# A reordered opening, tiled key transposes for the first unit, and counted filler products in a three-stage attention and MoE kernel

## The chip, the cores and the metric

The kernel runs on one core of one Trainium2 chip. The metric is the device time of one launch in microseconds (us); the time before is 801.66 us, the median of three runs (801.65 to 803.63). TensorE is called PE in the profile, VectorE DVE, ScalarE ACT, GpSimd POOL, and SP is the engine that issues nearly all DMAs.

## The reference

Three stages follow each other: a gated linear attention over 4 batches, 8 heads, 768 steps and head size 48; a feed-forward stage with `h*cos(h)` of width 2048; and a second one with a maximum over three products of width 768.

```python
# stage 1, per batch and head, step t (state is 48x48)
state = alpha[t][:, None] * state + outer(k[t], v[t])
y[t]  = q[t] @ state
# x = y of all heads side by side: 3072 tokens x 384
h = x @ w_in                      # 384 -> 2048
x = (h * cos(h)) @ w_out          # 2048 -> 384
h = maximum(maximum(x @ w1, x @ w2), x @ w3)   # 384 -> 768
out = h @ w_out2                  # 768 -> 384
```

## The kernel before

The 3072 tokens are worked in six units of 512 (`NU = 6`, `HB = 512`; eight chunks of 64 steps, two per batch). A unit has four pairs of heads; what the text calls a head below is one such pair, and unit 0 takes the last pair first.

`att(u, k, p, t0)` does one head of a unit in chunked form. Two scans on DVE make products of alpha: `g` backwards (L382 for unit 0, in two halves; L393 for the others) and its counterpart forwards (L388, L398), with a reciprocal between. POOL multiplies keys (L384, L397) and queries (L400) by them. PE transposes the keys (L405), ACT copies the transpose out (L408), PE makes the chunk scores (L417) and the key-value sums (L422), the scores are masked with the triangle `tri` (unit 0: ACT L429 and POOL L430; others: DVE L433), DVE updates the state (L443, L454; L440, L441), and `values` multiplies masked scores by values (L462) and queries by states (L469). A fp32 number is fed to the later stages as a high part and a low part (`fp32r`): ACT writes the high part (L498), and the low part is the remainder, made in unit 0 by a product with minus identity that adds to the PSUM bank (L501, then ACT L503), elsewhere by a DVE subtraction (L505). `pick` (L477) puts rows of the first head into the free rows 48 to 63 of the other three heads of unit 0.

`moe1(i)` is one of 96 tiles of the first feed-forward stage (16 per unit). Nine products in three groups of three, high by high, high by low, low by high (L525, L526, L527), make a 128x512 tile of `h`; ACT and DVE form `h*cos(h)` (L533, L534, L535, then L537 or L541), its high part (L538, L542) and low part (POOL L539 for tiles 0 to 19, DVE L547 from tile 20); and nine products in three groups (L552, L553, L554) add it to three PSUM accumulators `acc`. At the end of a unit each accumulator goes out through one buffer `yy`: ACT L561, DVE L562, a DMA, and only then the next. The accumulator can be used by the next unit once L562 has read it.

`weight(...)` brings a block of weights: a DMA of 384 KB of float64, ACT L322, DVE L323, the high part on ACT L327, and the low part on POOL (L331) or, for the blocks named in `LOD`, on DVE out of PSUM (L329). There are 32 blocks for the first feed-forward stage, alternating `w_in` and `w_out`.

The order of the instructions is not written by hand. Every operation is entered with an engine, a duration, what it reads and writes, and a due time. `Program.order` replays this list as a schedule, taking at each step the engine that is free first and its ready operation with the smallest due time, and the kernel is issued in that order; each engine then works its own queue in order and waits on semaphores. The table of constants at the head (`LIMIT`, `GLP1`, `LOD`, `W1E`, `ATT0`, `ATTS` and so on) and the duration formulas set due times, bank limits and engines.

Of the kernel before, what the change touches and what calls it, by code (L numbers as in the profile page):

```python
# [9 lines left out]
F32 = mybir.dt.float32  # L10
# [16 lines left out]
P = 128  # L27
C = 64
# [26 lines left out]
LIMIT = {"h": 3, "a": 3, "t": 1, "w": 1, "r": 2, "y": 2, "r0": 4}  # L55


RYS = 9
# [3 lines left out]
GLP1 = 20  # L62
# [15 lines left out]
WARM, COLD, IDLE = 16, 7.0, 2.5  # L78


class Program:
# [15 lines left out]
    def op(self, eng, dur, fn, reads=(), writes=(), due=0.0, nbytes=None, port=False):  # L97
# [19 lines left out]
        self.ops.append((eng, dur, nbytes, fn, sorted(deps), due, port))  # L117
        return n

    def order(self, banks, limit):  # L120
# [19 lines left out]
        free = dict.fromkeys(engines, 0.0)  # L140
# [8 lines left out]
        cold = COLD  # L149
        never = float("inf")  # L150
# [14 lines left out]
        for _ in range(n):  # L165
            t, e = min((max(free[e], min(map(ready, w))), e) for e, w in waiting.items() if w)
# [3 lines left out]
            _, dur, nbytes, _, _, _, port = self.ops[i]  # L170
            start[i] = t
            if e == "PE":
                if t - free[e] > IDLE:
                    cold = t + COLD
                dur += min(dur, max(0.0, cold - t) / 2)
            free[e] = t + dur
            end = t + dur
            if port:
                port_free = end
            if nbytes is not None:  # L180
                dma_free = max(dma_free, end + (0.65 if e == "SP" else 1.05)) + nbytes / 260e3
# [61 lines left out]
def tile_kernel(ctx, tc, aa, qk, vv, wt, outT):  # L243
# [29 lines left out]
    half_pi = mp.tile([P, 104], F32, name="pad1")[:, 0:1]  # L273
# [4 lines left out]
    v_b = [ap.tile([P, N2, 2, UP], F32, name=f"v{i}") for i in range(NV)]  # L278
# [30 lines left out]
    def weight(block, hi, lo, whi, wlo, due, extra=(), early=2.0):  # L309
# [4 lines left out]
        if wide:  # L314
# [6 lines left out]
            op("SP", HW, lambda: nc.sync.dma_start(raw[:, 1:1 + 4 * WB], wt[block].bitcast(U16)), (), [rk], due - early, dma(P * WB * 8))  # L321
# [30 lines left out]
    def att(u, k, p, t0):  # L352
# [6 lines left out]
        if u == 0 and k == 2:  # L359
            v, vk = q_b[2].rearrange("p (i j e) -> p i j e", i=N2, j=2), ("q", 2)  # L360
            kq_, kk_ = q_3.rearrange("p a b -> p (a b)")[0:PR, 0:2 * HB], "q01"
# [11 lines left out]
        op("SP", HW, lambda: nc.sync.dma_start(t, aa[u, p, :, 0:KO]), (), [kf], t0 - 4, dma(PR * KO * 4))  # L373
        op("SP", HW, lambda: nc.sync.dma_start(kq_, qk[u, p]), (), [kk, kq], t0 - 3.9, dma(PR * 2 * HB * 4))
        op("SP", HW, lambda: nc.sync.dma_start(v, vv[u, p]), (), [vk], t0 - 3, dma(P * HB * 4))
# [36 lines left out]
        def akmm():  # L412
            for i in range(N2):
                for h in range(2):
                    for j in range(2):
                        c, w = 2 * i + h, slice(UP * j, UP * j + D)
                        pe.matmul(r[j][C * h:C * (h + 1), AO + i * C:AO + (i + 1) * C], kv3[w, c], qv3[w, c], start=True, stop=True)  # L417
            for i in range(N2):
                for h in range(2):
                    for j in range(2):  # L420
                        w = UP if j == 0 else D
                        pe.matmul(r[h][UP * j:UP * j + w, i * D:(i + 1) * D], kt[C * h:C * (h + 1), i, UP * j:UP * j + w],  # L422
                                  v[C * h:C * (h + 1), i, j, 0:D], start=True, stop=True)

        op("PE", 2 * SWITCH + N2 * mm4(C) + N2 * mm4(D), akmm, [kk, kq, tk, vk, ("done", n2)], rk, t0 + 0.2)
# [18 lines left out]
        half = [slice(UP * h, UP * h + D) for h in range(2)]  # L444
# [11 lines left out]
        yks, y = ([("acc", 0), ("acc", 1)], acc[:2]) if u == 0 else psum2("r" if u <= RYS else "y")  # L456

        def values():
            for i in range(N2):
                for h in range(2):  # L460
                    for j in range(2):
                        pe.matmul(y[h][UP * j:UP * (j + 1), i * C:(i + 1) * C], v[C * h:C * (h + 1), i, j], a[C * h:C * (h + 1), j, i],  # L462
                                  start=(i == 0), stop=False, skip_group_check=True)
# [7 lines left out]
        picks = u == 0 and p < NP - 1  # L471

        def pick():
            for x in range(2):
                for h in range(2):
                    cs = slice(HB // 2 * h, HB // 2 * (h + 1))
                    pe.matmul(y[h][:, 0:HB // 2], sel[:, p], yy_b[0][:, x, cs], start=False, stop=False, skip_group_check=True)  # L477

        if picks:
            values_, values = values, lambda: (values_(), pick())  # L480
        op("PE", 2 * SWITCH + N2 * mm4(C) + N2 * mm4(C) + (0.7 if picks else 0.0), values,
           [*([("sel",), *[("yy0", x, h) for x in "hl" for h in range(2)]] if picks else []), vk, ("a", n2, 0), ("a", n2, 1), *[(dk, h) for h in range(0 if u else 1, 2)], *[("z", n2, h) for h in range(0 if u else 1, 2)], kq, kk], [*yks, ("done", n2)], t0 + 0.3)
# [12 lines left out]
        for h in range(2):  # L495
# [4 lines left out]
            if u < XLE:  # L500
                op("PE", 0.2, lambda h=h, cs=cs: pe.matmul(y[h][:, 0:HB // 2], minus, o()[:, 0, cs], start=False, stop=True, skip_group_check=True),  # L501
# [15 lines left out]
    def moe1(i):  # L517
# [17 lines left out]
        op("Act", act(HB), lambda: se.activation(q, q, AF.Sin, bias=half_pi), ["half pi"], [qk], m)  # L535
# [99 lines left out]
    def build():  # L635
# [17 lines left out]
        op("Pool", 1.0, lambda: make_identity(nc, ident), (), ["ident"], due=-99)  # L653
        def sine():
            ve.memset(half_pi, 0.5 * math.pi)
            se.activation(tri[:, 0, 0:1], half_pi, AF.Sin)

        op("Act", 1.4, sine, (), ["half pi", "tri"], due=-100)
# [19 lines left out]
        def warm():  # L678
            for _ in range(WARM):
                pe.matmul(acc[0][:, 0:P], ident, ident, start=True, stop=True)  # L680

        op("PE", 0.213 * WARM, warm, ["ident"], [("acc", 0)], due=-99)
# [120 lines left out]
```

## Time and profile before

| | before |
|---|---|
| median of three runs | 801.66 us |
| profiled execution, device time | 799.91 us |
| its span, first to last instruction | 798.2 us |
| PE busy | 778.7 us (98%) |
| DVE, ACT, POOL busy | 424.3, 359.6, 159.2 us |
| mean granted PE clock | 0.994 |
| moved by DMA | 71.44 MB, 90 GB/s |

A row of the timeline gives start, duration, engine, line, output and inputs, shapes, count, and in brackets the idle time before it with what ended it. Durations of matmuls overlap: the price of one in a dense stretch is the distance between two starts. Busy time counts work and not waits, and PE counts as busy while a matmul is in flight.

### The profile page before, as it was taken

The numbers are of one execution on the slowest core, as the hardware profiler recorded it, in microseconds if no ns is written. First come the engines' busy times: TensorE is split into PE (matmuls) and PEld (weight loads), VectorE is DVE, ScalarE is ACT, GpSimd is POOL, SyncE is SP. The second block draws the span as 40 slices with busy tenths as digits, with TensorE's granted clock in tenths as the row PEclk, the third lists the DMA queues.
The fourth block names the chain that finished last, engine by engine and source line by source line (L and its number), as shares of the span: only waits on it lengthen the run. The fifth ranks groups of instructions, "written<-read, shape, count | busy, mean of one in ns | idle before, by whom it ended". The sixth has DMA issues, their size and how long they took to land. (4 is left out here: it accounts for less than half of the span.)

```text
span 798.2 us, 14884 instructions
## 1 busy us (share of the span) xinstructions
PE 778.7 (98%) x6180; PEld 632.7 (79%) x6180; DVE 424.3 (53%) x701; ACT 359.6 (45%) x688; POOL 159.2 (20%) x155
## 2 busy tenths in 40 slices
PE   7899999999999999999999899999999999999998
PEld 7676777888788878878877688888888888888886
DVE  7689879756874686566567444532132222223221
ACT  5777757545654565455677344521111211112111
POOL 6667775301220122011233000200000000000000
PEclk9989999999999999999999999999999999999999
DMA  9668644501340143013256200502020110200001
GB/s 290 197 200 238 197 115 142 152 12 39 120 135 3 49 134 101 1 38 117 74 152 210 88 1 0 191 31 88 27 80 27 54 53 28 79 27 14 13 27 39
DMA packets 26466, 71.44 MB, mean 90 GB/s; under 512 B 3392, under 2 KB 3392, under 8 KB 26400
## 3 DMA queue, kind: packets, MB, share of 16 engines
q1 hardware_dynamic: 26400, 70.51, 27.9%
q8 instruction: 48, 0.79, 0.4%
q14 instruction: 18, 0.15, 0.1%
HBM read 54.37 MB, written 14.16 MB: 86 GB/s over the span
## 5 line engine op out<-in xcount | busy, mean ns | idle before, releaser
L552 PE MATMUL acc<-gh,woh 128*128 128x512 f32 x288 | 116.3, 404 | 2.6 <-DVE yy L562 2.2
L525 PE MATMUL ps<-xt,wih 128*128 128x512 f32 x288 | 116.0, 403 | 0.3 <-ACT wih L327 0.3
L554 PE MATMUL acc<-gl,woh 128*128 128x512 f32 x288 | 114.3, 397 | 0.5 <-POOL gl L539 0.5
L527 PE MATMUL ps<-xt,wil 128*128 128x512 f32 x288 | 113.3, 393 | 1.1 <-POOL wil L331 1.1
L553 PE MATMUL acc<-gh,wol 128*128 128x512 f32 x288 | 112.9, 392 | 0.0
L526 PE MATMUL ps<-xt,wih 128*128 128x512 f32 x288 | 112.8, 392 | 0.0
L535 ACT ACTIVATE q<-q,pad 128x512 f32<-128x512 f32 x96 | 69.3, 722 | 47.0 <-DVE q L534 46.8
L534 DVE SCALAR_TENSOR_TENSOR q<-q,ps 128x512 f32<-128x512 int32 x96 | 65.5, 683 | 37.3 <-ACT q L533 36.9
L613 DVE TENSOR_TENSOR ps<-t,ps 128x512 f32<-128x512 f32 x36 | 25.1, 696 | 104.4 <-PE ps L605 104.2
L533 ACT ACTIVATE q<-ps 128x512 int32<-128x512 f32 x96 | 57.0, 594 | 45.6 <-PE ps L527 44.9
L541 DVE TENSOR_TENSOR ps<-q,ps 128x512 f32<-128x512 f32 x76 | 52.8, 694 | 42.6 <-ACT q L535 42.1
L547 DVE TENSOR_TENSOR gl<-ps,gh 128x512 fp32r<-128x512 f32 x76 | 52.3, 689 | 42.9 <-ACT gh L542 42.5
L614 ACT ACTIVATE h<-ps 128x512 fp32r<-128x512 f32 x36 | 21.5, 598 | 109.7 <-DVE ps L613 109.7
L552 PEld LDWEIGHTS acc<-gh,woh 128*128 128x128 f32 x288 | 54.4, 189 | 16.2 <-DVE yy L562 4.2
L554 PEld LDWEIGHTS acc<-gl,woh 128*128 128x128 f32 x288 | 54.4, 189 | 15.7 <-DVE gl L547 2.5
L527 PEld LDWEIGHTS ps<-xt,wil 128*128 128x128 f32 x288 | 54.3, 189 | 14.2 <-POOL wil L331 2.6
L542 ACT ACTIVATE gh<-ps 128x512 fp32r<-128x512 f32 x76 | 45.1, 593 | 43.3 <-DVE ps L541 38.4
L525 PEld LDWEIGHTS ps<-xt,wih 128*128 128x128 f32 x288 | 54.5, 189 | 12.3 <-ACT wih L327 0.8
L611 DVE TENSOR_TENSOR t<-t,ps 128x512 f32<-128x512 f32 x36 | 24.7, 687 | 71.5 <-PE ps L605 70.8
L526 PEld LDWEIGHTS ps<-xt,wih 128*128 128x128 f32 x288 | 54.5, 189 | 10.3
L553 PEld LDWEIGHTS acc<-gh,wol 128*128 128x128 f32 x288 | 54.4, 189 | 10.3
L631 ACT ACTIVATE y<-ps 128x512 f32<-128x512 f32 x18 | 10.8, 597 | 93.2 <-PE ps L628 93.2
(151 smaller groups left out, 1508.0 us busy)
## 6 DMA issues: line engine op xcount, KB each, us to landing
raw<-in_wt SPq DMA_DIRECT2D x56, 384.0 KB, 3.6
kq<-in_qk SPq DMA_DIRECT2D x22, 448.0 KB, 4.2
x1d<-yy SPq DMA_DIRECT2D x18, 512.0 KB, 4.0
xt<-x1d SPq DMA_DIRECT2D x18, 512.0 KB, 4.3
v<-in_vv SPq DMA_DIRECT2D x23, 256.0 KB, 4.8
al<-in_aa SPq DMA_DIRECT2D x23, 228.4 KB, 2.7
outT<-y SPq DMA_DIRECT2D x18, 256.0 KB, 2.0
xt<-yy SPq DMA_DIRECT2D x30, 64.0 KB, 3.7
```

What stands on the lines that cost most here:

```text
L525: pe.matmul(ps, wi["h"][:, f, cc], xt[:, cc, 0], start=(cc == 0), stop=False)
L526: pe.matmul(ps, wi["h"][:, f, cc], xt[:, cc, 1], start=False, stop=False)
L527: pe.matmul(ps, wi["l"][:, f, cc], xt[:, cc, 0], start=False, stop=(cc == NR - 1))
L533: op("Act", act(HB, True), lambda: se.activation(q.bitcast(I32), ps, AF.Copy, bias=0.25, scale=INV2PI), [hk], [qk, *qx], m)
L534: op("DVE", dve(HB), lambda: ve.scalar_tensor_tensor(q, q.bitcast(I32), -TWOPI, ps, ALU.mult, ALU.add), [hk], [qk], m)
L535: op("Act", act(HB), lambda: se.activation(q, q, AF.Sin, bias=half_pi), ["half pi"], [qk], m)
L541: op("DVE", dve(HB), lambda: ve.tensor_tensor(ps, q, ps, ALU.mult), [qk], [hk], m)
L542: op("Act", act(HB, True), lambda: se.activation(gh, ps, AF.Copy), [hk], [("gh", gn)], m)
L547: op("DVE", dve(HB), lambda: ve.tensor_tensor(gl, ps, gh.bitcast(F32), ALU.subtract), [hk, ("gh", gn)], [("gl", gn)], m)
L552: pe.matmul(acc[c], oh, gh, start=(f == 0), stop=False)
L553: pe.matmul(acc[c], ol, gh, start=False, stop=False)
L554: pe.matmul(acc[c], oh, gl, start=False, stop=(f == NF1 - 1))
```

## The change

Parts of the diff:

- In unit 0 the keys are transposed by 16 products of 64x64 tiles with pieces of the identity, in the same tile mode as the scores, into two banks; two ACT copies of 192 columns replace one of 448. Other units keep the transpose.
- In unit 0 the scores are masked on DVE (`MKP` 0), and the low parts of its heads two to four are made by DVE (`XLE` counts heads now). The accumulators are used in alternating halves there, and `pick` comes before `values`.
- Values are loaded without padding (192 KB in place of 256 KB), and in unit 0 the DMA of the next alpha stands ahead of the values.
- The low parts of `w_in` move from POOL to DVE and those of `w_out` from DVE to POOL (`LOD`); the low parts of tiles 12 to 19 move from POOL to DVE (`GLP1`).
- Heads of later units are due 3.6 tiles apart in place of 2.5, weights two tiles earlier, and the replay has other prices (DMA, tile mode changes, unit 0 products).
- The sine takes its bias as a number. The warm-up has 14 products in place of 16, five of them half as wide, over all banks.
- Where the replay finds PE without work for over 0.55 us between 7.5 and 45 us, products of the identity (64 columns) are put in.

```diff
-LIMIT = {"h": 3, "a": 3, "t": 1, "w": 1, "r": 2, "y": 2, "r0": 4}
+LIMIT = {"h": 3, "a": 3, "t": 2, "w": 1, "r": 2, "y": 2, "r0": 4}
-RYS = 9
+RYS = 1
-GLP1 = 20
+GLP1 = 12
-MKP = 1
-GATE, GSTEP = 0, 1
-LOD = (1, 3)
-W1E = 10
-MOE_EARLY = 4
+MKP = 0
+GATE, GSTEP = 1, 3
+LOD = (0, 2)
+W1E = 12
+MOE_EARLY = 3
-FIRST = -40
-ATT0 = -3.0
-ATTS = 2.5
+FIRST = -12
+ATT0 = -2.0
+ATTS = 3.6
...
+            if e == "PE":
+                if tiled != mode:
+                    dur += SWITCH
+                    mode = tiled
...
+        first = FIRST - 20 + k if u == 0 else t0
+        op("SP", HW, lambda: nc.sync.dma_start(t, aa[u, p, :, 0:KO]), (), [kf], first - 4 - (0.8 if k else 0), dma(PR * KO * 4))
...
         def trans():
+            if u:
+                for i in range(N2):
+                    pe.transpose(pk[:, i * PR:(i + 1) * PR], kv[:, i * P:(i + 1) * P], ident[0:PR, 0:PR])
+                return
             for i in range(N2):
+                for h in range(2):
+                    for j in range(2):
+                        w = half[j]
+                        pe.matmul(pk[j][C * h:C * (h + 1), i * D:(i + 1) * D], kv3[w, 2 * i + h], ident[w, w], start=True, stop=True)
...
-            if u < MKP:
+            if u == 0 and k < MKP:
...
+            yks, y = [("acc", h, k % 2) for h in range(2)], [x[:, HB // 2 * (k % 2):] for x in acc[:2]]
...
-            if u < XLE:
+            if u * NP + k < XLE:
...
+    spare = {}
+    free = 0.0
+    for i in order:
+        if G.ops[i][0] == "PE":
+            t = start[i]
+            if IDLE0 < t < BUSY and t - free > 0.55:
+                spare[i] = int((t - free - 0.3) / 0.24)
+            free = t + G.ops[i][1]
     with tc.manual_schedule():
         for i in order:
+            for _ in range(spare.get(i, 0)):
+                pe.matmul(ps_b[NBANK - 1][:, 512 - C:], ident, ident[:, 0:C], start=True, stop=True)
             G.ops[i][3]()
```

How the instructions move is shown at three places. First DVE's queue around the scans of the fourth head of unit 0 (its products of alpha are written to `inv`, and `acc_98` holds the scans' seeds). Before:

```order
L382 SCALAR_TENSOR_TENSOR inv_124<-inv_123,acc_98 112x260 x2
L387 RECIPROCAL acc_98<-inv_124 112x4
L388 SCALAR_TENSOR_TENSOR inv_123<-inv_123,acc_98 112x260
L387 RECIPROCAL acc_98<-inv_124 112x4
L388 SCALAR_TENSOR_TENSOR inv_123<-inv_123,acc_98 112x260
```

The same place now:

```order
L401 SCALAR_TENSOR_TENSOR al_127<-al_127,acc_98 112x260
L458 TENSOR_TENSOR a_110<-ps_99,tri 128x256
L458 TENSOR_TENSOR a_110<-ps_100,tri 128x256
L468 TENSOR_TENSOR d_112<-ps_99,g_129 112x192
L400 RECIPROCAL acc_98<-inv_124 112x4
L478 TENSOR_TENSOR s_117<-ps_100,d_112 112x192
L401 SCALAR_TENSOR_TENSOR inv_123<-inv_123,acc_98 112x260
L334 SCALAR_TENSOR_TENSOR ps_103<-raw_89,top_93 128x384
L400 RECIPROCAL acc_98<-inv_124 112x4
L334 SCALAR_TENSOR_TENSOR raw_90<-raw_90,top_94 128x384
L401 SCALAR_TENSOR_TENSOR inv_123<-inv_123,acc_98 112x260
```

Two masks of the second head (L458) and two weight rows (L334) now stand ahead of the last scan; the two masks of the first head do so further up.

Second PE's queue at the first head of unit 1: its scores and the feed-forward groups ahead of them. Before (L405 is the transpose, L417 the scores):

```order
L525 MATMUL ps_103<-xt_425,wih 128x512
L526 MATMUL ps_103<-xt_425,wih 128x512
L527 MATMUL ps_103<-xt_425,wil 128x512
L525 MATMUL ps_103<-xt_425,wih 128x512
L526 MATMUL ps_103<-xt_425,wih 128x512
L527 MATMUL ps_103<-xt_425,wil 128x512
L405 MATMUL ps_101<-ident,kq_104 128x112 x4
L417 MATMUL ps_102<-kq_104 64x64
L417 MATMUL ps_99<-kq_104 64x64
```

The same place now (L775 is the filler, L444 the scores; the transpose stands six groups further up):

```order
L551 MATMUL ps_103<-xt_497,wih 128x512
L552 MATMUL ps_103<-xt_497,wih 128x512
L553 MATMUL ps_103<-xt_497,wil 128x512
L551 MATMUL ps_103<-xt_497,wih 128x512
L552 MATMUL ps_103<-xt_497,wih 128x512
L553 MATMUL ps_103<-xt_497,wil 128x512
L775 MATMUL ps_103<-ident 128x64 x7
L444 MATMUL ps_102<-kq_104 64x64
L444 MATMUL ps_101<-kq_104 64x64
```

Before, these scores stood behind the second feed-forward tile and ahead of the first `acc` products; now three tiles and seven fillers come first, a fourth tile follows, and then the `acc` products of two tiles.

Third ACT's queue at the last change of unit, between the copies of the second and third accumulator (`acc_97`, `acc_98`) into `yy`. Before:

```order
L561 ACTIVATE yy_88<-acc_97 128x512
L533 ACTIVATE q<-ps_102 128x512
L535 ACTIVATE q<-q,pad_95 128x512
L561 ACTIVATE yy_88<-acc_98 128x512
L542 ACTIVATE gh_83<-ps_101 128x512
```

The same place now:

```order
L587 ACTIVATE yy_88<-acc_97 128x512
L561 ACTIVATE q<-q 128x512
L559 ACTIVATE q<-ps_103 128x512
L338 ACTIVATE w2h<-raw_90 128x384
L333 ACTIVATE top_93<-raw_91 128x384
L561 ACTIVATE q<-q 128x512
L338 ACTIVATE w0h<-raw_91 128x384
L333 ACTIVATE top_93<-raw_89 128x384
L559 ACTIVATE q<-ps_101 128x512
L587 ACTIVATE yy_88<-acc_98 128x512
```

Eight instructions now stand between the two copies in place of two. On PE, one group in place of six stands between the last product into `acc_96` and the first into `acc_97` of the new unit, and seven groups in place of three between those into `acc_97` and `acc_98`.

## Rows read from the trace of the kernel before

**Rows 1.** Stretches: length, busy us (instructions) PE, PEld, DVE, ACT, POOL, PE clock, DMA.

```profile
16.00:21.00 5.00, 4.37 (x117) 4.10 (x118) 3.31 (x8) 2.53 (x7) 4.67 (x7) 0.66 1.06 347
37.50:45.00 7.50, 6.95 (x17) 5.12 (x18) 6.98 (x11) 4.11 (x8) 4.68 (x4) 0.54 0.33 109
...
60.00:100.00 40.00, 36.30 (x450) 27.98 (x449) 36.92 (x62) 31.11 (x63) 28.83 (x25) 1.00 0.72 216
100.00:150.00 50.00, 49.01 (x630) 38.64 (x629) 41.02 (x68) 32.80 (x67) 31.28 (x27) 1.00 0.48 140
...
52.15:163.40 111.25, 106.50 (x1348) 83.66 (x1348) 92.85 (x157) 76.84 (x156) 70.54 (x62) 1.00 0.58 171
```

**Rows 2.** Timeline of PE, opening.

```profile
1.43 6.62 PE L680 MATMUL acc<-ident 128*128 128x128 f32 x32 [1.43 <-POOL ident masks.py:199]
...
8.36 0.69 PE L417 MATMUL ps<-kq 48*64 48x64 f32 x32
9.06 0.68 PE L422 MATMUL ps<-v,kt 64*64 64x48 f32 x32
...
29.90 0.74 PE L477 MATMUL acc<-yy,gl 128*128 128x256 f32 x4
...
36.52 0.68 PE L422 MATMUL ps<-v,kt 64*64 64x48 f32 x32 [1.09 <-ACT kt L408]
...
38.88 0.80 PE L554 MATMUL acc<-gl,woh 128*128 128x512 f32 x1 [0.54 <-POOL gl L539]
...
43.31 0.63 PE L525 MATMUL ps<-xt,wih 128*128 128x512 f32 x1
43.74 0.63 PE L526 MATMUL ps<-xt,wih 128*128 128x512 f32 x1
...
45.41 0.39 PE L552 MATMUL acc<-gh,woh 128*128 128x512 f32 x1
```

**Rows 3.** Timeline of DVE.

```profile
3.58 1.28 DVE L382 TENSOR_TENSOR_SCAN g<-al,acc 112x260 f32<-112x260 f32 x2 [0.43 <-DMA al<-in_aa]
...
17.63 0.69 DVE L388 TENSOR_TENSOR_SCAN inv<-inv,acc 112x260 f32<-112x260 f32 x1
...
25.38 0.56 DVE L323 SCALAR_TENSOR_TENSOR ps<-raw,top 128x384 uint32<-128x384 uint32 x1
...
38.71 0.75 DVE L433 TENSOR_TENSOR a<-ps,tri 128x256 f32<-128x256 f32 x2
...
51.47 0.68 DVE L534 SCALAR_TENSOR_TENSOR q<-q,ps 128x512 f32<-128x512 int32 x1
...
162.70 0.69 DVE L534 SCALAR_TENSOR_TENSOR q<-q,ps 128x512 f32<-128x512 int32 x1 [0.55 <-ACT q L533]
```

**Rows 4.** Timeline of POOL, then one row of ACT, opening.

```profile
18.40 1.18 POOL L400 TENSOR_TENSOR yy<-yy,inv 112x512 f32<-112x512 f32 x1 [0.33 <-DVE inv L388]
...
37.54 1.28 POOL L539 TENSOR_TENSOR gl<-q,gh 128x512 fp32r<-128x512 f32 x1 [3.00 <-ACT gh L538]
...
31.48 0.66 ACT L503 ACTIVATE xt<-acc 128x256 fp32r<-128x256 f32 x2 [0.27 <-PE acc L501]
```

**Rows 5.** Timeline of PE in the full stretch, behind a head's tiled products.

```profile
201.13 0.50 PE L525 MATMUL ps<-xt,wih 128*128 128x512 f32 x1
201.47 0.39 PE L526 MATMUL ps<-xt,wih 128*128 128x512 f32 x1
201.70 0.40 PE L527 MATMUL ps<-xt,wil 128*128 128x512 f32 x1
```

**Rows 6.** Page, costliest groups: count, busy us and mean ns.

```profile
L547 DVE TENSOR_TENSOR gl<-ps,gh 128x512 fp32r<-128x512 f32 x76 | 52.3, 689 | 42.9 <-ACT gh L542 42.5
```

**Rows 7.** Timeline at the last change of unit: ACT, then PE.

```profile
444.36 0.58 ACT L561 ACTIVATE yy<-acc 128x512 fp32r<-128x512 f32 x1
450.32 0.60 ACT L561 ACTIVATE yy<-acc 128x512 fp32r<-128x512 f32 x1 [3.19 <-DMA x1d<-yy]
...
451.70 0.50 PE L552 MATMUL acc<-gh,woh 128*128 128x512 f32 x1 [2.17 <-DVE yy L562]
```

More of the change, by code (lines that the diff above doesn't have):

```diff
@@ L139, in order @@
         engines = sorted({o[0] for o in self.ops})
[L140 removed]
+        free = dict.fromkeys(engines, 0.8)
         waiting = {e: [] for e in engines}
@@ L149, in order @@
         cold = COLD
+        mode = False
         never = float("inf")
@@ L165, in order @@
         for _ in range(n):
-            t, e = min((max(free[e], min(map(ready, w))), e) for e, w in waiting.items() if w)
+            _, e, t = min((t - (0.1 if e == "Pool" else 0.0), e, t) for e, t in (
+                (e, max(free[e], min(map(ready, w)))) for e, w in waiting.items() if w))
             assert t < never
@@ L277, in tile_kernel @@
     kq_b = [ap.tile([PR, 2 * HB], F32, name=f"kq{i}") for i in range(NKQ)]
-    v_b = [ap.tile([P, N2, 2, UP], F32, name=f"v{i}") for i in range(NV)]
+    v_b = [ap.tile([P, N2, 2, D], F32, name=f"v{i}") for i in range(NV)]
     a_b = [ap.tile([P, 2, N2, C], F32, name=f"a{i}") for i in range(2)]
@@ L372, in att @@
         ik, tk, dk, sk = ("iv", n2), ("kt", n2), ("d", n2), ("s", p)
-        op("SP", HW, lambda: nc.sync.dma_start(t, aa[u, p, :, 0:KO]), (), [kf], t0 - 4, dma(PR * KO * 4))
-        op("SP", HW, lambda: nc.sync.dma_start(kq_, qk[u, p]), (), [kk, kq], t0 - 3.9, dma(PR * 2 * HB * 4))
-        op("SP", HW, lambda: nc.sync.dma_start(v, vv[u, p]), (), [vk], t0 - 3, dma(P * HB * 4))
+        half = [slice(UP * h, UP * h + D) for h in range(2)]
+        first = FIRST - 20 + k if u == 0 else t0
+        op("SP", HW, lambda: nc.sync.dma_start(t, aa[u, p, :, 0:KO]), (), [kf], first - 4 - (0.8 if k else 0), dma(PR * KO * 4))
+        op("SP", HW, lambda: nc.sync.dma_start(kq_, qk[u, p]), (), [kk, kq], first - 3.9, dma(PR * 2 * HB * 4))
+        op("SP", HW, lambda: nc.sync.dma_start(v, vv[u, p]), (), [vk], first - 3.7, dma(P * HB * 3))
         if u == 0:
@@ L420, in akmm @@
                     for j in range(2):
[L421 to L425, printed above, removed]
+                        pe.matmul(r[h][half[j], i * D:(i + 1) * D], kt[C * h:C * (h + 1), i, UP * j:UP * j + D], v[C * h:C * (h + 1), i, j], start=True, stop=True)
+        op("PE", slow * N2 * (mm4(C) + mm4(D)), akmm, [kk, kq, *tks, vk, ("done", n2)], rk, t0 + 0.2 if u else t0 - 0.9, tiled=True)
         for j in range(2):
             rv = r[j][:, AO:AO + N2 * C].rearrange("p (c t) -> p c t", c=N2)
-            if u < MKP:
+            if u == 0 and k < MKP:
                 op("Act", act(HB // 2, True), lambda j=j, rv=rv: se.activation(a[:, j], rv, AF.Copy), [rk[j]], [("a", n2, j)], t0 + 0.2)
@@ L454, in att @@
             op("DVE", dve(N2 * D), lambda: ve.tensor_tensor(s, kvs[1], d[:, 1], ALU.add), [rk[1], (dk, 1)], [sk], t0 + 0.27)
-        yks, y = ([("acc", 0), ("acc", 1)], acc[:2]) if u == 0 else psum2("r" if u <= RYS else "y")
+        picks = u == 0 and p < NP - 1
+        if u:
+            yks, y = psum2("r" if u <= RYS else "y")
+        else:
+            yks, y = [("acc", h, k % 2) for h in range(2)], [x[:, HB // 2 * (k % 2):] for x in acc[:2]]
         def values():
@@ L461, in values @@
                     for j in range(2):
-                        pe.matmul(y[h][UP * j:UP * (j + 1), i * C:(i + 1) * C], v[C * h:C * (h + 1), i, j], a[C * h:C * (h + 1), j, i],
-                                  start=(i == 0), stop=False, skip_group_check=True)
+                        pe.matmul(y[h][half[j], i * C:(i + 1) * C], v[C * h:C * (h + 1), i, j], a[C * h:C * (h + 1), j, i],
+                                  start=(i == 0 and not picks), stop=False, skip_group_check=True)
             for i in range(N2):
@@ L476, in pick @@
                     cs = slice(HB // 2 * h, HB // 2 * (h + 1))
-                    pe.matmul(y[h][:, 0:HB // 2], sel[:, p], yy_b[0][:, x, cs], start=False, stop=False, skip_group_check=True)
+                    pe.matmul(y[h][:, 0:HB // 2], sel[:, p], yy_b[0][:, x, cs], start=(x == 0), stop=False, skip_group_check=True)
         if picks:
-            values_, values = values, lambda: (values_(), pick())
-        op("PE", 2 * SWITCH + N2 * mm4(C) + N2 * mm4(C) + (0.7 if picks else 0.0), values,
-           [*([("sel",), *[("yy0", x, h) for x in "hl" for h in range(2)]] if picks else []), vk, ("a", n2, 0), ("a", n2, 1), *[(dk, h) for h in range(0 if u else 1, 2)], *[("z", n2, h) for h in range(0 if u else 1, 2)], kq, kk], [*yks, ("done", n2)], t0 + 0.3)
+            op("PE", slow * 0.5, pick, [("sel",), *[("yy0", x, h) for x in "hl" for h in range(2)]], yks, t0 + 0.28)
+        op("PE", slow * N2 * 2 * mm4(C), values,
+           [vk, ("a", n2, 0), ("a", n2, 1), *[(dk, h) for h in range(0 if u else 1, 2)], *[("z", n2, h) for h in range(0 if u else 1, 2)], kq, kk], [*yks, ("done", n2)], t0 + 0.3, tiled=True)
         xa = []
@@ L534, in moe1 @@
         op("DVE", dve(HB), lambda: ve.scalar_tensor_tensor(q, q.bitcast(I32), -TWOPI, ps, ALU.mult, ALU.add), [hk], [qk], m)
-        op("Act", act(HB), lambda: se.activation(q, q, AF.Sin, bias=half_pi), ["half pi"], [qk], m)
+        op("Act", act(HB), lambda: se.activation(q, q, AF.Sin, bias=0.5 * math.pi), (), [qk], m)
         if GLE1 <= i < GLP1:
@@ L652, in build @@
         op("DVE", 1.3, setup_pads, (), ["one0", *(("top", i) for i in range(NTOP))], due=-30)
-        op("Pool", 1.0, lambda: make_identity(nc, ident), (), ["ident"], due=-99)
+        op("Pool", 0.55, lambda: make_identity(nc, ident), (), ["ident"], due=-99)
         def sine():
-            ve.memset(half_pi, 0.5 * math.pi)
-            se.activation(tri[:, 0, 0:1], half_pi, AF.Sin)
-        op("Act", 1.4, sine, (), ["half pi", "tri"], due=-100)
+            ve.memset(sin0, 0.0)
+            se.activation(sin0, sin0, AF.Sin, bias=0.5 * math.pi)
+        op("Act", 1.4, sine, (), (), due=-100)
         op("Act", act(P), lambda: se.activation(minus, ident, AF.Copy, scale=-1.0), ["ident"], ["minus", ("gl", 1)], due=-98)
@@ L678, in warm @@
         def warm():
-            for _ in range(WARM):
-                pe.matmul(acc[0][:, 0:P], ident, ident, start=True, stop=True)
-        op("PE", 0.213 * WARM, warm, ["ident"], [("acc", 0)], due=-99)
+            for i, x in enumerate((*acc[:2], *ps_b)):
+                pe.matmul(x[:, 0:P], ident, ident, start=True, stop=True)
+                n = C if i > 1 else P
+                pe.matmul(x[:, P:P + n], ident, ident[:, 0:n], start=True, stop=True)
+        op("PE", WARM, warm, ["ident"], [("acc", 0, 0), ("acc", 1, 0)], due=-99)
         events = []
```

47 lines of the change are left out of this document (27 added, 20 removed).

## The prediction

> **What bounds the kernel now.** I read the page's table of engines first: PE is busy 98% of the span, so only its idle time, its slow clock and the work given to it can move the end. [...] Last the timelines: PE's first products, the groups of three of the feed-forward stage, and what each waits for.
>
> At the slow clock two starts lie 0.43 us apart [rows 2], at the full one 0.23 [rows 5]. A group of three is 0.69 us. By 45.41 us [rows 2] PE has done nine groups of `h` (three tiles) and three `acc` groups (one tile), twelve in all, and the scores of the first head of unit 1.
>
> Both orders hold nearly the same sequence on PE from feed-forward tile 18 on. So the change is worth what PE has gained when the sequences meet, plus what differs at the last change of unit.
>
> **The opening, step by step.** The heads of unit 0 hang on DVE's scans. Before, they begin at 3.58 and the last ends at 17.63 + 0.69 = 18.32 us [rows 3]. Now two pairs of masks (2 x 0.75) and two weight rows (2 x 0.56) stand ahead of that last scan [rows 3]: it ends near 18.32 + 2.6 = 20.9. That part of the change costs time. POOL's product follows (0.15 and 1.18 [rows 4]) to 22.2, the scores and sums take 8.36 to 9.74, 1.4 us [rows 2], to 23.7. The masks that came from ACT and POOL before now wait in DVE's queue behind one low part (0.56), masks and two state sums of the third head (0.75, and 0.7 as an estimate by their width of 192 against the masks' 256), two low halves (as a mask pair, 0.75) and two weight rows (1.1), to 24.8; then the two masks with a weight's low part between, whose high part ACT must write first, and the state product end near 27.3. An ACT copy and the last half of the products bring the fourth head to 28.4, against 29.90 where its last products end and `pick` begins [rows 2]. 1.5 us are gained here, since the accumulators' halves alternate and PE no longer waits for the subtraction products.
>
> The low halves of this head come behind more on DVE: I put them at 31.7, where ACT's were done at 31.48 + 0.66 = 32.14 [rows 4]. By then PE has four groups behind it. Five groups follow to 35.1, the seven fillers (half a warm-up product each record, 6.62/32 = 0.21 us for each filler [rows 2]) to 36.6, the scores to 38.0, three groups to 40.0. The first `acc` group needs a low part: before, POOL's first ran from 37.54 for 1.28 us and PE waited for it [rows 4, 2]. DVE, ACT and POOL now have three tiles in hand and serve the first two together; I add 2.9 us for the longer queues and put it at 41.7. From there sixteen products end two tiles of `acc` at 45.3.
>
> So at 45.3 us PE has 18 groups behind it instead of 12 at 45.41: 6 x 0.69 + 0.1 = **4.2 us**. Some 3.4 of it are the slow clock of 37.5 to 45 us, 7.5 x 0.46 [rows 1]: its slow stretch began after waits of about 1 us for a transpose copy [rows 2], which no longer stand there, and the work from 25 us on is denser. The cover is bounded: if the clock falls again, 3.4 us of the 4.2 are gone; if every wait for low parts went too, 1.5 more are won.
>
> **Tile modes.** Behind tiled products the next start lies 0.34 us off, not 0.23 [rows 5]: a change of mode costs 0.11. Three lots of fillers add six changes, 0.7 us at most; they stand where PE waits in any case, so I take 0. [...]
>
> **From 43 to 163 us: DVE.** Between the 4th and the 24th cosine reduction (L534, at 51.47 and 162.70 [rows 3]) DVE was busy 92.85 of 111.25 us, 83% [rows 1]. By the order it now has, between the same two: eight more low parts (0.69 each [rows 6]), 5.5; one more pair of long scans, taken as four short halves, 2.6; one more weight with its low part, 1.1; two masks, two low halves and two state sums fewer, -2.2: about 100 us. In that stretch one head less is worked by PE, about 2.9 us (its scores and sums 1.4, its values the same, a short transpose); it comes later. The 4th reduction ends near 43.1 by the chain above. If PE keeps its 4.2 us, the 24th ends at 163.4 - 4.2 - 2.9 = 156.3. DVE then needs 100 in 113.2 us, 88%, between the 83% of this stretch and the 92% that it reached from 60 to 100 us. I take PE's waits there as unchanged, **0**, since the share asked for lies in the middle. Bounds: at 92% DVE would be done in 108.3, 4.9 us sooner (PE's waits of 4.7 us in [rows 1] are about that); at the 82% of 100 to 150 us it takes 122, 8.8 us later.
>
> **The last change of unit.** PE waited 2.17 us [rows 7] for an accumulator: the copies at 444.36 and 450.32 share one buffer, and the second waits for the DMA. Now seven groups (4.8 us) in place of three stand between the products into these two, so this wait goes; but only one group, not six, covers the wait for the accumulator ahead of it, whose copy has to come some 3 us sooner and stands only two places earlier in ACT's queue. I take 1 us of the 2.2, so **-1.0**, between -2.2 and +1.5.
>
> **Counted at nothing.** Unpadded values: 64 KB less of 256 on each load; before 45 us the loads set less than DVE does, and later the DMA share is 0.48 to 0.72 [rows 1]; bounds -0.5 and 0. The subtraction products removed (six, PE waiting anyway): the same. The sine's bias as a number: same shape, ACT is busy 77 of 111 us [rows 1]; 0, bounds 1 us each way. The swap of low parts between POOL and DVE: the same count on DVE; POOL, 70.5 of 111 busy, gets lighter by the eight that it loses.
>
> **Sum.** 4.2 + 0 + 1.0 = 5.2 us off a span of 798.2: 793.0, and with the 1.7 us around the span 794.7 for such an execution. The profiled execution (799.91) was 1.75 below the median, so against the median 801.66 - 5.2 = **796.5**.
>
> **Rivals.**
> 1. DVE runs as densely as from 60 to 100 us. For it: the masks of unit 0 are done when DVE had time, heads are spread wider, POOL does less. Against it: chains between ACT and DVE leave DVE idle when tiles come one by one. 4.9 us more: 791.6.
> 2. The clock falls in the new opening too: the products of unit 0 are as sparse as before in 10 to 25 us, and DVE's longer queue leaves PE waiting ahead of the first low part. Fillers then don't do what they are for. 3.4 us of the gain go: 799.9.
> 3. Slower: DVE becomes the bound. It has 7 us more work in the stretch, and PE's queue holds every `h` group behind a weight's low part that is now DVE's (0.56 us behind scans of over 1 us) instead of POOL's. At 82% it ends 8.8 us later: 796.5 + 8.8 = 805.3. It decides below 100/(113.2 + 5.2) = 84.5%: from there the change loses.
>
> **How the numbers follow.** A difference under 0.3%, 2.4 us, is what a measurement of this kernel can't tell from none. Forecast 0.46 (its own range 793.5 to 799.5), rival 1 0.20, rival 2 0.14, rival 3 0.15, and 0.05 for the rest. Faster: 0.43 of the forecast, 0.20, 0.05 of rival 2: 0.68. Slower: most of rival 3 and part of the rest, 0.14. The same: 0.18. The range reaches from beyond rival 1 to short of rival 3's point, 789.5 to 803.5.
>
> **What would show it.** Right: 18 groups done near 45 us at clock 1.00 from 25 us on; DVE's last scan of unit 0 at 20 to 21.5; DVE near 88% between the 4th and 24th reductions, PE's waits from 50 to 150 us near 5 us; no wait over 1.5 us at the last change of unit. Wrong: a clock near 0.5 between 30 and 50 us (rival 2); PE waiting over 8 us for low parts `wil` or `gl` from DVE (rival 3), or under 2 us (rival 1).

## The result, and the profile after

The changed kernel takes 794.11 us (median of 5 runs, 793.08 to 796.71) against 801.66: the ratio is 0.9908, with a 95% interval of 0.9883 to 0.9933. The forecast was 796.5. The steps behind it came out otherwise than forecast, and that their errors nearly cancel is luck.

The stretches of the changed kernel, in the columns of [rows 1], and last the one between its 4th and 24th cosine reductions:

```profile
16.00:21.00 5.00, 3.94 (x120) 3.63 (x124) 1.95 (x7) 1.94 (x6) 1.72 (x2) 0.62 1.06 346
21.00:37.50 16.50, 14.02 (x331) 11.59 (x324) 11.73 (x29) 10.63 (x27) 6.10 (x7) 0.80 0.70 210
37.50:45.00 7.50, 5.31 (x44) 4.35 (x46) 5.48 (x9) 7.45 (x16) 3.21 (x3) 0.97 0.54 151
45.00:60.00 15.00, 15.00 (x175) 12.34 (x168) 10.91 (x21) 8.82 (x19) 8.40 (x9) 0.90 0.46 134
60.00:100.00 40.00, 38.63 (x346) 29.93 (x345) 29.39 (x55) 30.87 (x63) 26.15 (x25) 1.00 0.65 195
100.00:150.00 50.00, 49.90 (x696) 39.31 (x695) 44.32 (x82) 31.23 (x66) 19.73 (x21) 1.00 0.49 149
50.79:158.59 107.80, 106.33 (x1235) 83.66 (x1234) 90.11 (x165) 74.66 (x153) 53.41 (x52) 1.00 0.55 164
```

Against [rows 1], the slow clock of 37.5 to 45 us is gone (0.97 for 0.54), but PE now idles 2.2 of those 7.5 us, and the clock is low before and behind it. From 60 to 150 us PE waits 1.5 us instead of 4.7. DVE is not denser there: 90.1 of 107.8 us, 84%, where it was 83%.

PE's opening in the changed kernel (start, length, engine, line, idle time before and what ended it):

```profile
17.06 0.25 PE L497 MATMUL acc<-kq,d 48*48 48x64 f32 x1 [3.14 <-issue]
...
23.38 0.56 PE L426 MATMUL ps<-ident,yy 48*64 48x48 f32 x9 [1.92 <-issue]
...
42.83 1.77 PE L775 MATMUL ps<-ident 128*128 128x64 f32 x14 [2.19 <-DVE wil L340]
...
49.21 0.40 PE L578 MATMUL acc<-gh,woh 128*128 128x512 f32 x1
```

Two waits of 3.1 and 1.9 us have no releaser: the profile shows nothing that PE waits for. The last seven fillers wait 2.2 us for a weight's low part, because the bank that they write (one of the five PSUM tiles `ps`) holds that weight. The first `acc` product comes at 49.21 us behind 12 groups of `h`; before, 12 groups were done at 45.41 [rows 2]. At the last change of unit one short wait is left where 2.17 us stood [rows 7]:

```profile
438.30 0.50 PE L578 MATMUL acc<-gh,woh 128*128 128x512 f32 x1 [0.40 <-DVE yy L588]
```

**Where the time went.** From each trace I work out PE's idle and slow time: the time passed, less 0.2268 us for each feed-forward product started, less the heads' products and transposes at what they take between 200 and 400 us. The 16 transposes that tiled products replace in unit 0 are allowed for (1.3 us). In us:

```
                          to 50  50-150  150-430  430-460  rest  heads' products   span
before                     27.4    11.8      7.9      3.5   3.9             50.2  798.2
changed                    31.2     6.8      7.4      1.0   3.9             47.6  791.3
a_att                      31.4    15.0      8.9      1.0   4.3             47.8  801.7
a_fill40                   28.7     7.4      7.2      1.0   3.8             47.6  789.3
a_nofill                   27.8     8.0      8.4      0.7   4.0             47.7  790.1
p_nofill                   28.5     6.9      7.5      1.0   3.8             47.7  788.8
n_att                      27.8    16.5      7.2      0.1   4.0             47.9  796.9
n_lod                      27.7    12.6      7.7      0.7   3.8             47.6  793.6
p_mkp                      33.7     9.9      8.1      1.0   3.9             47.8  797.8
p_tr                       26.6     7.9      7.3      0.8   4.2             47.7  787.8
p_trw                      28.7     7.7      8.1      0.7   4.2             47.7  790.6
b_mids                     29.9     8.8      8.9      5.1   3.9             50.2  800.3
b_sine                     28.3    11.8      7.0      4.1   3.8             50.2  798.8
b_unpad                    26.9    11.9      7.7      4.8   3.9             47.7  796.4
```

The span fell by 6.9 us: the opening lost 3.8, 50 to 150 us gained 5.0, 150 to 430 gained 0.5, the last change of unit 2.5, and the heads' products became 2.6 us shorter. One profiled execution stands behind each row; up to 50 us two executions of nearly one order (before, b_sine) differ by 0.9. The one of n_att (798.58 us) is the fastest of its twelve, 4.4 below their median.

### The profile page after: what moved, and what is told of

Same layout as the page of the kernel before. It is cut to its first block, busy times and chain, and to the rows that moved or that the text cites. A ratio compares the mean times of both kernels' runs of the same rounds, so it can differ in the third digit from the quotient of the medians.

```text
span 791.3 us, 15142 instructions
## 1 busy us (share of the span) xinstructions
PE 776.0 (98%) x6320; PEld 634.8 (80%) x6320; DVE 421.0 (53%) x723; ACT 348.8 (44%) x678; POOL 136.1 (17%) x139
## 5 line engine op out<-in xcount | busy, mean ns | idle before, releaser
L561 ACT ACTIVATE q<-q 128x512 f32<-128x512 f32 x96 | 60.5, 630 | 43.8 <-DVE q L560 43.8
L567 DVE TENSOR_TENSOR ps<-q,ps 128x512 f32<-128x512 f32 x84 | 58.1, 692 | 37.7 <-ACT q L561 37.5
L573 DVE TENSOR_TENSOR gl<-ps,gh 128x512 fp32r<-128x512 f32 x84 | 57.7, 687 | 34.6 <-ACT gh L568 33.9
L568 ACT ACTIVATE gh<-ps 128x512 fp32r<-128x512 f32 x84 | 50.0, 595 | 42.4 <-DVE ps L567 40.8
L553 PEld LDWEIGHTS ps<-xt,wil 128*128 128x128 f32 x288 | 54.2, 188 | 11.8 <-DVE wil L340 0.3
```

Of the source, the lines that this page charges most:

```text
L553: pe.matmul(ps, wi["l"][:, f, cc], xt[:, cc, 0], start=False, stop=(cc == NR - 1))
L567: op("DVE", dve(HB), lambda: ve.tensor_tensor(ps, q, ps, ALU.mult), [qk], [hk], m)
```

## The experiments

**Fillers, spread of the heads, the middle alone, the sine alone.** First the changed kernel without fillers:

```
-            if IDLE0 < t < BUSY and t - free > 0.55:
+            if False:
```

> The changed kernel without its fillers (products of the identity that no output reads). Theory A (the opening costs time, the middle pays): the fillers neither hold the clock nor hide, and the 14 records ahead of 42.83 us stand in the way of a cosine reduction; without them 12 groups of h are done about 1 us sooner and the time is 793 to 794.5 us. Theory B (the fillers do what the forecast let them do): without them the clock of the opening is near 0.54 for some 7 us longer, 3.4 us more: 797.5.

791.86 us, ratio 0.9871 (0.9846 to 0.9896). Theory A, and more than it said: PE's idle and slow time up to 50 us falls from 31.2 to 27.8 us, and 12 groups of `h` are done at 45.8 instead of 49.2. The clock of 0 to 16 us is 0.81 to 0.94 in the seven runs of the changed kernel without fillers and 0.92 to 1.00 in the three with them; from 21 to 37.5 us it is 0.66 to 0.80 and 0.51 to 0.80. Fillers don't hold it where it counts.

```
-ATT0 = -2.0
-ATTS = 3.6
+ATT0 = -3.0
+ATTS = 2.5
```

> The changed kernel with the heads of unit 1 and later spread as before (ATT0 -3.0, ATTS 2.5). Theory A1 (the wider spread is what takes PE's waits of 50 to 150 us away): these waits come back, some 6 us of 9; 800 us, with about 8 us of waits of PE between 50 and 150 us. Theory A2 (the low parts on DVE and the shorter sine on ScalarE took them away): 794 to 796, waits near 3 us.

803.29 us, ratio 1.0007 (0.9988 to 1.0026): A1, and more than it said; 15.0 us between 50 and 150. In this build the bank of the last seven fillers held an `h` tile, of which they overwrite 64 of 512 columns before its product with the cosine; that one tile isn't the reference's. n_att, below, has the same edit without fillers.

```
-GLP1 = 20
+GLP1 = 12
...
-LOD = (1, 3)
-W1E = 10
-MOE_EARLY = 4
+LOD = (0, 2)
+W1E = 12
+MOE_EARLY = 3
...
-ATT0 = -3.0
-ATTS = 2.5
+ATT0 = -2.0
+ATTS = 3.6
```

These are the changed kernel's numbers in the kernel before; the sine's bias is a number here too.

> The kernel before with its own opening (masks on ScalarE and GpSimd, padded values, transposes, no fillers) and the rest of the constants of the changed one (LOD, GLP1, W1E, MOE_EARLY, ATT0, ATTS) and the sine's bias as a number. Theory A (the middle gained about 8 us and the last change of unit 2, the new opening lost about 4): 12 groups done at 45.4 us and 790 to 792 us. Theory B (as forecast: the opening gains 4.2, the middle nothing): 800 to 802 us. If only the heads' new opening lets the middle run without waits, in between, 796.

800.62 us, ratio 0.9992 (0.9971 to 1.0014). The time is theory B's, its reason isn't: the middle does gain, 11.8 to 8.8 us, but the same numbers make this opening 2.5 us longer and the last change of unit 1.6. The gain of the middle can't be had from these numbers alone.

```
-... se.activation(q, q, AF.Sin, bias=half_pi), ["half pi"], [qk], m)
+... se.activation(q, q, AF.Sin, bias=0.5 * math.pi), (), [qk], m)
```

> The kernel before with the sine's bias as a number instead of a column of a tile, nothing else. Theory A (the sine gets 0.09 us shorter but lies beside PE's work): 630 ns a sine instead of 722, and 801 to 802.5 us. Rival (the chain of ScalarE and VectorE sets the waits between 50 and 113 us, and each shorter sine is one part of what the middle gained): 798 to 799.5 us.

800.45 us, ratio 0.9976 (0.9961 to 0.9991), some 1.9 us less (0.7 to 3.1), between the two theories: a sine takes 631 ns, but 50 to 150 us holds 11.8 us of waits as before. Where the 1.9 us come from its one profile doesn't show.

**Unpadded values alone, fillers once more, spread and low parts without fillers.** In the kernel before, the narrower stationary operands:

```
-                        w = UP if j == 0 else D
-                        pe.matmul(r[h][UP * j:UP * j + w, ...], kt[..., i, UP * j:UP * j + w], ...)
+                        pe.matmul(r[h][UP * j:UP * j + D, ...], kt[..., i, UP * j:UP * j + D], ...)
...
-                        pe.matmul(y[h][UP * j:UP * (j + 1), ...], v[...], ...)
+                        pe.matmul(y[h][UP * j:UP * j + D, ...], v[...], ...)
```

> The kernel before with unpadded values only (and the same 32 warm-up products spread over all banks, so that the rows the narrower products leave out hold numbers). Theory A (each of a head's blocks on PE got shorter by the narrower values: in the changed kernel 0.98 and 1.04 us instead of 1.07 and 1.07 between 200 and 400 us): the two blocks shorten in the same way, 24 heads x 0.11 = 2.7 us less, ratio near 0.9966. Theory B (as forecast, unpadded values are worth nothing; the blocks shortened because the row positions of their results changed with the new order): blocks as before and a ratio of 1.000.

798.57 us, ratio 0.9953 (0.9934 to 0.9971): theory A. A head's scores and sums in the full stretch, before and then in this run (PE's timeline):

```profile
211.93 0.69 PE L417 MATMUL ps<-kq 48*64 48x64 f32 x32
212.44 0.62 PE L422 MATMUL ps<-v,kt 64*64 64x48 f32 x32
212.99 0.50 PE L525 MATMUL ps<-xt,wih 128*128 128x512 f32 x1
```

```profile
209.96 0.69 PE L417 MATMUL ps<-kq 48*64 48x64 f32 x32
210.47 0.54 PE L421 MATMUL ps<-v,kt 64*48 64x48 f32 x32
210.94 0.50 PE L523 MATMUL ps<-xt,wih 128*128 128x512 f32 x1
```

The scores keep their 0.51 us; the 32 sums, whose stationary tile is 64 columns wide for half of them before and 48 now, take 0.47 instead of 0.55. With the values (1.073 to 1.043 us) that is 0.11 us a head, 2.6 for 24.

```
-IDLE0, BUSY = 7.5, 45.0
+IDLE0, BUSY = 7.5, 40.0
```

> The changed kernel without the fillers that the plan puts behind 40 us; the earlier ones stay. Theory A (only the last lot costs: it overwrites a bank that a cosine reduction still reads, and PE waited 2.2 us for that): no such wait near 40 us, PE's idle and slow time up to 50 us about 29 us instead of 32.5, time as without any fillers, ratio 0.986 to 0.988. Theory B (the earlier lots cost too, or the gain without fillers was chance): 0.990 or above.

790.92 us, ratio 0.9861 (0.9843 to 0.9879). The edit missed its aim: by the plan's own clock the last lot lies ahead of 40 us, and all fillers stayed. What differs is the banks. The planner hands them out among equals in the order in which a set of names is walked, and that differs from build to build. Here the fillers' bank held an `h` tile whose reduction ended in time (64 columns of it are overwritten and wrong, as in a_att):

```profile
41.89 1.33 PE L775 MATMUL ps<-ident 128*128 128x64 f32 x10 [0.21 <-DVE q L560]
```

So the wait of 2.19 us at 42.83 belongs to one build of the changed kernel: its opening is 31.2 us with it, 28.7 here with all fillers and no such wait. That theory A's figures came out is no proof of A.

n_att is a_att's edit without fillers; n_lod, also without fillers, has

```
-LOD = (0, 2)
+LOD = (1, 3)
```

> The changed kernel without fillers and with the heads of unit 1 and later spread as before (ATT0 -3.0, ATTS 2.5). Theory A1 (the wider spread took PE's waits of 50 to 150 us away, the fillers have no part in it): PE's idle and slow time between 50 and 150 us rises from 8 to 14 to 16 us, time 797 to 800 us. Theory A2 (the low parts on VectorE did): it stays at 7 to 9 us, and the time at 791 to 793.

> The changed kernel without fillers and with the other two of three low parts on VectorE (LOD back to (1, 3)), so that the first weight's low part comes from GpSimd again. Theory A1 (spread of the heads decides): PE's idle and slow time between 50 and 150 us stays at 7 to 9 us, time 791 to 793. Theory A2 (where the low parts stand decides): it rises by 3 to 5 us, time 795 to 797.

n_att: 802.94 us, ratio 1.0000 (0.9982 to 1.0017). n_lod: 795.96 us, 0.9927 (0.9909 to 0.9945). PE's share in 60 to 100 and 100 to 150 us, n_att first:

```profile
60.00:100.00 40.00, 34.89 (x381) 26.76 (x379) 28.64 (x50) 27.26 (x56) 24.26 (x23) 0.96 0.51 149
100.00:150.00 50.00, 46.22 (x688) 36.52 (x679) 43.77 (x80) 32.22 (x69) 17.88 (x19) 1.00 0.55 160
```

```profile
60.00:100.00 40.00, 35.16 (x329) 27.30 (x327) 29.34 (x53) 30.89 (x62) 26.21 (x24) 1.00 0.59 181
100.00:150.00 50.00, 47.96 (x686) 37.47 (x686) 46.10 (x81) 28.75 (x62) 19.61 (x20) 1.00 0.48 143
```

Neither theory holds alone: without the wider spread the stretch of 50 to 150 us has 8.5 us more of PE's idle and slow time, without the moved low parts 4.6 more. With both old (the kernel before) it is 11.8, with both new 6.8 to 8.0, with one of them old 16.5 or 12.6: either gains only together with the other. In n_att PE waits while DVE is busy only 28.6 of 40 us, ACT 27.3 and POOL 24.3: it isn't waiting on a full engine. That bunched heads leave it waiting on their chain through the three is my reading.

**The opening's parts, with the banks pinned.** p_nofill repeats a_nofill with one line changed:

```
-        for k in {*reads, *writes}:
+        for k in dict.fromkeys((*reads, *writes)):
```

> The changed kernel without fillers once more, with one line changed in its planner: equal candidates for a bank are taken in the order in which they are named, not in the order in which a set is walked, which differs from build to build. Theory A (without fillers the five banks are interchangeable): as the run without fillers before it, ratio 0.987, PE's idle and slow time 29 us up to 50 us and 8 us from 50 to 150. Theory B (the choice of banks by itself is worth as much as the steps argued over): a ratio off by 0.004 or more.

791.50 us, ratio 0.9877 (0.9857 to 0.9898): theory A: 0.4 us from a_nofill's 791.86. Without fillers the choice of banks shows no difference beyond the intervals.

p_tr is p_nofill with unit 0's keys transposed as those of the other units are, four transposes and one copy a head:

```
-        pk_k, pk = psum("t") if u else psum2("t")
+        pk_k, pk = psum("t")
...
-            if u:
+            if True:
                 for i in range(N2):
                     pe.transpose(pk[:, i * PR:(i + 1) * PR], kv[:, i * P:(i + 1) * P], ident[0:PR, 0:PR])
...
-        if u:
+        if True:
```

> As p_nofill, but the keys of unit 0 transposed as those of the others are (16 transposes and one copy a head, in place of 128 tiled identity products and two copies a head). Theory A (the opening hangs on VectorE's scans and masks, the products lie beside them): PE's idle and slow time up to 50 us within 0.5 us of p_nofill's, after 1.3 us for the 16 transposes is allowed for; time within 1 us. Theory B (the tiled products cost PE time ahead of the first scores, at the slow clock): 1.5 to 3 us less.

789.36 us, ratio 0.9835 (0.9813 to 0.9857), the fastest kernel of the study: theory B by its number, 1.9 us less up to 50 us than p_nofill. Its reason isn't shown alone: p_nofill stands still for 2.0 us behind its 222nd product, and p_tr, with fewer products ahead, has no such stop (the last section has these stops).

p_mkp is p_nofill with the masks of unit 0 on ACT and POOL:

```
-MKP = 0
+MKP = 4
```

> As p_nofill, but the masks of unit 0 on ScalarE and GpSimd as before instead of on VectorE. Theory A (the masks on VectorE put its last scan of unit 0 from 18.3 to 23.2 us and the opening hangs on that): the last scan ends near 19 us, PE's idle and slow time up to 50 us falls by 1.5 to 2.5 us. Theory B (as forecast, the masks come 1.5 us sooner from VectorE in all, since GpSimd takes 1.2 us for one): it rises by 1 to 2 us.

799.31 us, ratio 0.9972 (0.9958 to 0.9987): the sign is theory B's, the size, 5.2 us more up to 50 us, is beyond it, and the trace shows another reason. DVE's last scan does end at 18.2 us, and the heads of unit 0 are no later with the masks on ACT and POOL: PE's first feed-forward group starts at 31.36 us (32.40 in p_nofill), its seventh at 39.75 (39.49). A mask takes GpSimd 0.73 us (median of the eight in the kernel before, 0.72 to 1.50), not 1.2. The loss comes behind them, at the first head of unit 1. The plan now puts that head's scans later in DVE's queue, the second at 45.53 us (37.77 in p_nofill), and PE waits for the copy of its transpose and for its queries. First DVE, then PE:

```profile
17.49 0.69 DVE L401 TENSOR_TENSOR_SCAN inv<-inv,acc 112x260 f32<-112x260 f32 x1
...
45.53 1.23 DVE L411 TENSOR_TENSOR_SCAN al<-al,inv 112x520 f32<-112x520 f32 x1
```

```profile
31.36 0.63 PE L551 MATMUL ps<-xt,wih 128*128 128x512 f32 x1
...
45.37 0.50 PE L551 MATMUL ps<-xt,wih 128*128 128x512 f32 x1 [2.01 <-ACT kt L430]
...
48.78 1.14 PE L444 MATMUL ps<-kq 48*64 48x64 f32 x32 [2.30 <-POOL kq L413]
```

**The waits without a releaser.** p_trw is p_tr with fewer, wider warm-up products:

```
-                pe.matmul(x[:, 0:P], ident, ident, start=True, stop=True)
-                n = C if i > 1 else P
-                pe.matmul(x[:, P:P + n], ident, ident[:, 0:n], start=True, stop=True)
+                pe.matmul(x[:, 0:3 * P]..., ident, ident[:, None, :].to_broadcast([P, 3, P]), ...)
```

> As p_tr, with the 28 warm-up products of PE's start drawn together into 14 wider ones that take about as long; every later instruction is the same, but stands 14 products earlier in PE's stream. In all runs so far PE stood still for 0.9 to 3.4 us behind its 221st or 222nd and its 347th to 349th product, whatever these were, with no semaphore to wait for; in p_tr 3.4 us behind the 348th, the 7th of the 32 scores of the last head of unit 0. Theory A (PE's instructions arrive in portions of some 127 products, over the DMA queues that the loads fill): the stall stays behind the 348th product, which is now the 21st of these scores. Theory B (that place of the program waits for something the profile doesn't show): it stays behind the 7th score, now the 334th product. Time by either within 1 us of p_tr's, 788 to 790 us.

791.40 us, ratio 0.9874 (0.9851 to 0.9898). The last head's scores on PE, p_tr first:

```profile
21.83 0.29 PE L444 MATMUL ps<-yy 48*64 48x64 f32 x4
25.34 0.62 PE L444 MATMUL ps<-yy 48*64 48x64 f32 x25 [3.22 <-issue]
```

```profile
21.31 0.55 PE L444 MATMUL ps<-yy 48*64 48x64 f32 x17
26.64 0.58 PE L444 MATMUL ps<-yy 48*64 48x64 f32 x10 [4.78 <-issue]
```

Theory A: counted in the trace, the stop stays behind the 348th product of PE's stream, now 14 scores later. The time was expected within 1 us of p_tr's and is 2.0 above: the stop ends 1.3 us later. That all runs show both stops without a semaphore, as expected above, isn't so; the last section has the count.

## Why the forecast came out as it did

- **The opening, -4.2 us forecast, +3.8 measured: the step that failed most.** I followed the heads over DVE, POOL and ACT and gave PE no stops and no slower clock than before. DVE's last scan ended at 23.2 us, not 20.9, since DVE waited 3.13 us for scores that stood behind PE's first stop. The fourth head's low halves ended at 36.3, not 31.7 (before: 32.14): PE stood still again until 23.38, its clock was 0.56 from 16 to 26 us (before: 0.83), and the fourth head's scores began at 28.67, not 22.2. The first `acc` group began at 49.21, not 41.7, behind the fillers' wait and a clock of 0.70 from 45 to 50 us. DVE, then PE, in the changed kernel:

```profile
19.05 0.76 DVE L458 TENSOR_TENSOR a<-ps,tri 128x256 f32<-128x256 f32 x2 [3.13 <-PE ps L448]
...
22.46 0.69 DVE L401 TENSOR_TENSOR_SCAN inv<-inv,acc 112x260 f32<-112x260 f32 x1
...
35.56 0.75 DVE L531 TENSOR_TENSOR xt<-acc,xt 128x256 fp32r<-128x256 f32 x2
```

```profile
28.67 0.69 PE L444 MATMUL ps<-yy 48*64 48x64 f32 x32
```

  The slow clock of 37.5 to 45 us did vanish, but the 3.4 us counted for it were taken back earlier: the clock is 0.62 and 0.80 in 16 to 37.5, where it was 0.66 and 1.00. The runs price two parts. The fillers' wait for a bank costs 2.5 to 3.4 us (31.2 against 28.7 with the wait absent and 27.8 without fillers): I put fillers at 0, and weighed only their mode changes. The tiled key products cost 1.9 us (p_nofill against p_tr), with the stop that they bring: I gave them no price. Without both (p_tr) the opening is still only 0.8 us shorter than before; a stop of 3.2 us and a clock of 0.79 from 21 to 37.5 us stay there, and no run separates these two. Rival 2 named the clock and the fillers rightly, but put the slow clock at 30 to 50 us, where it was mostly 16 to 30, and its 3.4 us are less than half of the 8.0. That masks of unit 0 on DVE bring its heads sooner isn't shown: p_mkp loses its 5.2 us at unit 1.
- **43 to 163 us, 0 forecast, -5.0 measured.** Two steps failed. The term mis-sized is DVE's 100 us: it needed 90.1. And PE's waits don't follow DVE's share, as the term had it: from 50 to 150 us DVE is busy 86.6 us before, 83.0 in the changed kernel and 81.2 in n_att, and PE's idle and slow time is 11.8, 6.8 and 16.5. DVE's counts were right (11 low parts for 3, nine pairs of scans for eight), the durations were not: I took those of a kernel in which GpSimd was busier beside them. DVE's shapes between 50 and 160 us, before and then changed (count, busy us, mean ns):

```profile
L393 DVE TENSOR_TENSOR_SCAN g<-al,one 112x520 f32<-112x520 f32 x8 | 11.9, 1486 | 0.0
L398 DVE TENSOR_TENSOR_SCAN al<-al,inv 112x520 f32<-112x520 f32 x8 | 11.8, 1474 | 0.1
L323 DVE SCALAR_TENSOR_TENSOR raw<-raw,top 128x384 uint32<-128x384 uint32 x14 | 12.5, 891 | 0.9 <-ACT top L322 0.5 <-issue 0.2
L441 DVE TENSOR_TENSOR d<-s,g 112x192 f32<-112x192 f32 x8 | 4.5, 566 | 0.1
```

```profile
L406 DVE TENSOR_TENSOR_SCAN g<-al,one 112x520 f32<-112x520 f32 x9 | 11.5, 1272 | 0.0
L411 DVE TENSOR_TENSOR_SCAN al<-al,inv 112x520 f32<-112x520 f32 x9 | 11.1, 1234 | 0.0
L334 DVE SCALAR_TENSOR_TENSOR raw<-raw,top 128x384 uint32<-128x384 uint32 x14 | 9.0, 645 | 0.2 <-POOL wol L342 0.2
L466 DVE TENSOR_TENSOR d<-s,g 112x192 f32<-112x192 f32 x7 | 2.8, 399 | 0.0
```

  The same shapes are 14 to 30% shorter: 9 x (0.21 + 0.24) + 14 x 0.25 + 7 x 0.17 = 8.7 us, of which 12 weight rows that land in PSUM (560, now 634 ns) give 0.9 back. GpSimd's share of its stretch fell from 63% [rows 1] to 50%. Taken one by one in all 14 traces, from 50 to 160 us, a long scan that no GpSimd instruction overlaps takes 1.18 to 1.24 us, a weight row (L323, L334) 0.51 to 0.57 and L441's shape 0.31 to 0.36; beside GpSimd they take up to 2.3, 1.7 and 1.4. State sums of 192 columns that read PSUM take 0.32 to 0.36 either way. What makes the others longer beside GpSimd isn't shown. Rival 1 had the size (4.9) and its sign came (PE waits 1.5 us from 50 to 150, under 2), but not its mechanism: DVE was not denser, it had less to do. Rival 3 didn't come. The wider spread, which I had named only in the rival's favour, and the moved low parts carry the gain together (n_att, n_lod); no run shows how much of it DVE's shorter work is.
- **Unpadded values, 0 (bounds -0.5 and 0) forecast, -2.6 measured.** I priced their loads and not PE's narrower stationary tiles; b_unpad shows them alone.
- **The last change of unit, -1.0 forecast (-2.2 to +1.5), -2.5 measured.** The wait for the shared buffer went, as forecast: 0.1 to 1.0 us in all builds of the new order, 3.5 to 5.1 in those of the old. Which of the order's changes did it no run takes out alone; b_mids and b_unpad show that the constants and the unpadded values don't do it by themselves.
- **The sine, 0 (1 us each way) forecast**; b_sine gives -0.7 to -3.1.
- **Sum.** 8.0 us too hopeful in the opening; too cautious by 5.0 in the middle, 2.6 on values, 1.5 at the change of unit and 0.6 elsewhere: 1.7 us net, with the span 6.9 shorter instead of 5.2. Of the signs named, only "no wait over 1.5 us at the last change" came as the forecast had it.

## What to carry to other kernels

When work leaves an engine beside which another one's instructions took longer (here long scans on DVE, up to 2.3 us beside GpSimd and 1.18 to 1.24 alone), take the other's durations from a stretch where its neighbour was quiet, not from the crowded one. Price an edit on every engine that reads the changed operand: with 48 stationary columns in place of 64 for half of them, 32 tiled products took 0.47 us instead of 0.55, and fillers whose bank was held waited 2.19 us. In an opening whose loads fill the DMA queues (share 1.06 from 16 to 21 us) count PE's products, not only its busy time: it stood still for 3.1 and 1.9 us behind the 222nd and the 349th.

## What the runs showed of the hardware that was not expected

- **PE stands still behind the same counts of products.** Counted in the 14 traces, from start to start, PE stands still for 0.9 to 5.0 us behind the 221st or 222nd product of its stream in 11 and behind the 347th to 349th in 13, whatever these products are. In four of the 11 (before, b_mids, b_sine, p_mkp) the profile names a releaser. In p_tr from 14 to 15 us the DMA queues' list has

```profile
q1 hardware_dynamic: 149, 0.24, 103.2%
q8 instruction: 1, 0.02, 7.2%
```

  one packet of the queue `instruction` among loads that fill all of the DMA engines' time. The next starts in the microsecond from 22 in p_tr, from 23 in p_trw and from 20 in the changed kernel, and the stops end at 25.3, 26.6 and 23.4. It is so everywhere: each of the 24 stops, those with a named releaser too, ends 1.2 to 1.6 us behind the end of such a packet (16 KB). From one stop to the next are 127 products before (221 to 348) and in the changed kernel (222 to 349); with 14 products fewer ahead, p_trw's second stop stays behind the 348th. That PE's instructions come in portions with these packets, theory A of p_trw, agrees with the counts and the ends; what a packet carries isn't shown.
- **With its bias as a number the sine took 631 ns instead of 722.** The sine's rows on the page, b_sine and then before, 128x512 both:

```profile
L535 ACT ACTIVATE q<-q 128x512 f32<-128x512 f32 x96 | 60.6, 631 | 46.4 <-DVE q L534 46.1
```

```profile
L535 ACT ACTIVATE q<-q,pad 128x512 f32<-128x512 f32 x96 | 69.3, 722 | 47.0 <-DVE q L534 46.8
```

  91 ns each with nothing else changed in the instruction.
